# Attention and two MLPs on one core: the second q's pieces over five units, and the weight conversions' buffers

## The chip, the cores and the metric

The kernel runs on one core of a Trainium2 chip. Its time is the device time of one execution in microseconds (us); lower is better. The engines are named as in the profile: PE (TensorE, matmul) with PEld (its weight loads), DVE (VectorE), ACT (ScalarE), POOL (GpSimd) and SP (SyncE, which here only issues DMAs).

## The reference, cut to what matters

```python
q, k, v: (4, 8, 576, 64)                       # batch, heads, sequence, head size
q_rot, k_rot = rotate(q), rotate(k)            # x1*cos - x2*sin, x1*sin + x2*cos
scores = q_rot @ k_rot.T / 8
attn = exp(scores - max(scores));  attn = attn / (sum(attn) + 1e-9)
x = (attn @ v), heads side by side             # (2304, 512)
h = x @ w_in                                   # (512, 2048), float64 in memory
g = where(h >= 1, h, where(h <= -1, 0, (h + 1)**2 / 4));  x = g @ w_out
h = x @ w_in2;  g = s * max(h, 0)**2 + b;      out = g @ w_out2
```

## The kernel before

**Precision.** Matmuls run on a rounded 32-bit format, and each operand is split into a high part (rounded) and a low part (the rest), so that a product is three matmuls: high by high, high by low, low by high. The weights of both MLPs come as 64-bit floats. `convert` makes the two parts out of a half slice of 128x512: ACT scales the upper words into the tile `wa` (L134); four DVE instructions (L135 to L138) build the 32-bit word in `wm` and the scaled rest in `wa`; ACT rounds `wm` into the high part (L139); POOL then takes `wm` minus the high part, written back to `wm`, and adds `wa` into the low part. A helper cuts each POOL operation into two pieces of 256 columns (all have line 96). `wa` and `wm` have one buffer each, the raw words (`wraw`) have two.

**Attention.** It runs over 16 pairs of heads, each of 9 units, so over units 0 to 143. A unit is: PE makes the scores (L357, `sc`), DVE takes their negated maximum (L359, `nm`), ACT takes the exponential (L364, `p`), PE transposes `p` (L379, `tp`), ACT or DVE copies that out (`pt`), PE multiplies by v (L405, `av`). Per pair, `rope_pair` rotates the q and the k of the next pair: POOL multiplies by the table (`qin<-qin,tab_sb`, `kin<-kin,tab_sb`), DVE or POOL adds, `lay_q` (ACT L308 and DVE L309) writes q's high and low parts into `qs`, and the k goes by DMA. For q of the second pair (pair 1) the rotation is DVE's (L292, L294), in two halves of 288 columns at units 2 and 3. The result of a pair is written in two groups to `u` (two buffers) and stored with one DMA.

**The fill.** From unit 48 on, matmuls of the first MLP (`h`, `y`, L181) on batches that are done stand between the units. The conversions for them are asked for from unit 33 on (every second unit) and from unit 70 on (every fourth), and may move up to 14 units earlier; from unit 96 on, eight more are parked in memory. After the attention follow the rest of the first MLP (`hps`, `yps`) and the second one (`sum`, `yps`).

**What sets the order.** During the attention a scheduler puts the instructions of each engine in a fixed order when the program is built, from its own idea of their durations; an engine then works through its list strictly in that order. `issue_after` ties an instruction behind another one of the same engine. After the attention PE's order is the order of the code.

Of the kernel before, what the change touches and what calls it, by code (L numbers as in the profile page):

```python
# [8 lines left out]
F32 = mybir.dt.float32  # L9
# [5 lines left out]
ALU = mybir.AluOpType  # L15
# [4 lines left out]
B, H, S, D = 4, 8, 576, 64  # L20
# [3 lines left out]
P = 128  # L24
NP = H // 2
# [41 lines left out]
def kernel(ctx, tc, qq, kk, vv, tab, ww1, ww2, s, b, out):  # L67
# [28 lines left out]
            m = nc.gpsimd.tensor_tensor(out=out[c], in0=in0[c], in1=in1[c], op=op)  # L96
        return m

    made = []

    def split(dst_hi, dst_lo, src, hi_eng, lo_eng):
        if hi_eng is nc.scalar:
# [12 lines left out]
    class Slice:  # L115
# [6 lines left out]
        def convert(self, raw, pools, hi, lo):  # L122
            if not wide:
                split(hi, lo, raw, nc.scalar, nc.gpsimd)
                return


            top = raw.bitcast(F32).rearrange("p (n t) -> p n t", t=2)[:, :, 1]
            low = raw.bitcast(U16).rearrange("p (n t) -> p n t", t=4)[:, :, 1]
            pool = pools[self.f * 2 + self.made & 1 if len(pools) > 1 else 0]  # L130
            a = pool.tile([P, HW], F32, tag="wa", name="wa", bufs=WB)
            m = pool.tile([P, HW], F32, tag="wm", name="wm", bufs=WB)
            au, mu = a.bitcast(U32), m.bitcast(U32)
            nc.scalar.activation(a, top, AF.Copy, scale=2.0 ** -112)  # L134
            nc.vector.tensor_scalar(out=mu, in0=au, scalar1=3, scalar2=None, op0=ALU.logical_shift_left)  # L135
            nc.vector.scalar_tensor_tensor(out=mu, in0=au, scalar=0x80000000, in1=mu, op0=ALU.bitwise_and, op1=ALU.bitwise_or)
            nc.vector.tensor_scalar(out=au, in0=mu, scalar1=0xFF800000, scalar2=None, op0=ALU.bitwise_and)
            nc.vector.scalar_tensor_tensor(out=a, in0=low, scalar=2.0 ** -36, in1=a, op0=ALU.mult, op1=ALU.mult)  # L138
            nc.scalar.copy(hi, m)  # L139
            pool_tt(out=m, in0=m, in1=hi, op=ALU.subtract)  # L140
            pool_tt(out=lo, in0=m, in1=a, op=ALU.add)

        def load(self, stage, k):
            raw = stage.tile([P, HW], self.ww.dtype, tag="wraw", name="wraw", bufs=RB)
# [94 lines left out]
    g1p = p1.enter_context(tc.tile_pool(name="g1p", bufs=GB1, reuse_waits="tile"))  # L239
    att = pa.enter_context(tc.tile_pool(name="att", bufs=1, side="right", reuse_waits="tile"))  # L240
    att2 = pa.enter_context(tc.tile_pool(name="att2", bufs=2, side="right", reuse_waits="tile"))
    ps_s = pp.enter_context(tc.tile_pool(name="ps_s", bufs=2, space=PSUM))
    ps_b = pp.enter_context(tc.tile_pool(name="ps_b", bufs=4 - BF, space=PSUM))
    ps_f = pp.enter_context(tc.tile_pool(name="ps_f", bufs=BF, space=PSUM)) if BF else ps_b
# [180 lines left out]
    def finish(i, g, e, eb, slices):  # L425
        ps = bank("av")
        for kts in slices:
            av(i, g, ps, kts)
            if 3 not in kts:
                yield  # L430
        rm = bank("rm")
        for t in range(2):
            nc.tensor.transpose(rm[:, t * P:(t + 1) * P], eb[:, 2 * t:2 * t + 2, :].rearrange("p j d -> p (j d)"), ident)
        if g == 0:
            nc.tensor.transpose(rm[:, 256:384], e[:, 4:5].to_broadcast([P, P]), ident)
            u_t[i] = att2.tile([P, S], F32, tag="u", name="u")
        r = att2.tile([P, 384], F32, tag="r", name="r", bufs=1)
        nc.scalar.copy(r[:, :384 - 128 * g], rm[:, :384 - 128 * g])
        u = u_t[i]
        c = slice(256 * g, 256 * g + 256)  # L440
        nc.vector.tensor_tensor(out=u[:, c], in0=ps[:, :256], in1=r[:, :256], op=ALU.mult)
        if g == 0:
            nc.vector.tensor_tensor(out=u[:D, 512:], in0=ps[:D, 256:320], in1=r[:D, 256:320], op=ALU.mult)
            nc.vector.tensor_tensor(out=u[D:, 512:], in0=ps[D:, 256:320], in1=r[D:, 320:384], op=ALU.mult)
            return
        bb, hp = divmod(i, NP)
        nc.sync.dma_start(out=xd[hp, :, bb * S:(bb + 1) * S], in_=u_t.pop(i))
# [26 lines left out]

    kept, begun = set(), set()

    def beside(work):
        x = split_x(work[0][0], work[0][0] in kept)
        for _ in range(LEAD):
            yield 1.0  # L480
        for n, (c, gi) in enumerate(work):
            grp = set_a[gi * G1:(gi + 1) * G1]
            gs = []
            for sl in grp:
                while sl.made < 1:
                    sl.half(wst, scratch)
                ps = ps_f.tile([P, 512], F32, tag="bank", name="h")
                accumulate(ps[:, :N1], h_terms(sl.w, *x), CF)
                gs.append(act1(ps[:, :N1], N1, ac1, g1p, nc.vector if c < GE else nc.gpsimd))
                if c not in kept:  # L490
                    kept.add(c)
                    keep_parts(x, c * N1, N1)
                yield 1.0
            if n + 1 < len(work) and work[n + 1][0] != c:
                x = split_x(work[n + 1][0], work[n + 1][0] in kept)
            for sl in grp:
                while sl.made < 2:
                    sl.half(wst, scratch)
            for d in range(KD):
                at = slice(c * N1, (c + 1) * N1)  # L500
                if c in begun:
                    yq = m2.tile([P, N1], F32, tag="yq", name="yq", bufs=2)
                    nc.sync.dma_start(out=yq, in_=yd[0, d, :, at])
                ps = ps_f.tile([P, 512], F32, tag="bank", name="y")
                accumulate(ps[:, :N1], y_terms([sl.w for sl in grp], gs, d), CF)
                y = m2.tile([P, N1], F32, tag="ys", name="ys")
                nc.scalar.copy(y, ps[:, :N1])  # L507
                if c in begun:
                    pool_tt(out=yq, in0=y, in1=yq, op=ALU.add)
                    y = yq  # L510
                nc.sync.dma_start(out=yd[int(c in begun), d, :, at], in_=y)
                yield 1.0
            begun.add(c)
# [71 lines left out]
    def do_load(n):  # L585
# [10 lines left out]
        if n < len(units):  # L596
            i, k = units[n]
            if i + 1 < NPAIR:
                if i == 0 and k in (2, 3):
                    with tc.issue_after(maxs[k]):  # L600
                        rope_pair(1, "q", nc.vector, nc.vector, None, HALVES[k - 2:k - 1])
                if i and k == 0:
                    with ExitStack() if i > 1 else tc.issue_after(parts[1][1]), ExitStack() if i > 1 else tc.issue_after(maxs[8]):
                        rope_pair(i + 1, "q", nc.gpsimd, nc.vector, None)
                elif k == 2:
                    with ExitStack() if i else tc.issue_after(exps[2]), ExitStack() if i else tc.issue_after(lowest):
# [24 lines left out]
    def do_av(n):  # L631
# [7 lines left out]
        while todo:  # L639
            i, k, steps = todo[0]  # L640
            with tc.issue_after(tps[n - LT]) if n < NS else ExitStack():
                more = next(steps, True)
            if more is None:
                if n < NS:
                    break
                continue
            todo.pop(0)
            if k == 8 and (i + 1) % NP == 0 and i // NP < B - 1:
                fill.append(beside(ORDERS[i // NP]))

    def do_fill(n):
        if n < 48:
# [10 lines left out]
                acts[o](n)  # L663
    while fill:
        run_fill(1.0)
    pa.close()
    pp.close()
    p1.close()
# [532 lines left out]
```

## Time and profile before

| | us |
|---|---|
| runs | 1116.85, 1114.28, 1115.39 |
| median | 1115.39 |
| the profiled execution: time | 1117.7 |
| the profiled execution: span from first to last instruction | 1115.9 |
| PE busy in the span | 1076.5 (96%) |
| DVE, ACT, POOL busy | 779.3, 629.0, 428.1 |
| attention and fill on PE end at about | 442 |

The profiled execution is 2.3 us above the median. PE's idle time lies almost entirely in the first 280 us and in the last few. A PE that is shown busy is not a PE at its peak, since the ends of matmuls are modelled. The granted clock is TensorE's, as a share of its higher level.

### The profile page before, as it was taken

How to read it: one execution, taken by the hardware profiler on the slowest of the kernel's cores; microseconds unless marked ns; L12 is line 12 of the kernel's file. 1: busy time of each engine (PE TensorE's matmuls, PEld its weight loads, DVE VectorE, ACT ScalarE, POOL GpSimd, SP SyncE). 2: the span in 40 equal slices, each digit the busy share in tenths (PEclk: the TensorE clock that was granted, in tenths of full speed). 3: DMA queues.
4: the chain of work that ended last, by engine and by line, in shares of the span. 5: the costliest groups of instructions: out<-in, count | busy, mean ns of one | idle time of the engine just before them, and what ended most of it. 6: DMA issues, size and time to landing. Idle time of an engine off the chain costs nothing.

```text
span 1115.9 us, 20048 instructions
## 1 busy us (share of the span) xinstructions
PE 1076.5 (96%) x7296; PEld 983.0 (88%) x7296; DVE 779.3 (70%) x1453; ACT 629.0 (56%) x1432; POOL 428.1 (38%) x564
## 2 busy tenths in 40 slices
PE   3999999989999999999999999999999999999998
PEld 3776778868888889999999999999999999999997
DVE  7889987878676663444757667866787778677754
ACT  5677776767666665554545455474554448334431
POOL 6889987676473232332544445110212110000000
PEclk9999999999999999999999999999999999999999
DMA  8466856656675554645455663231322844221210
GB/s 240 146 194 178 256 169 204 187 161 205 203 228 161 171 165 134 224 171 187 151 180 207 213 226 122 91 108 64 113 90 90 303 158 127 83 82 43 80 63 36
DMA packets 109762, 173.24 MB, mean 155 GB/s; under 512 B 29408, under 2 KB 80608, under 8 KB 109664
## 3 DMA queue, kind: packets, MB, share of 16 engines
q1 hardware_dynamic: 109664, 171.97, 48.4%
q8 instruction: 57, 0.93, 0.4%
q14 instruction: 41, 0.34, 0.1%
HBM read 110.10 MB, written 48.56 MB: 142 GB/s over the span
## 4 chain that ended last, share of the span: by engine, by line
PE 83%; DVE 6%; ACT 3%; POOL 3%; issue 2%; DMA 2%; SPq 0%; POOLq 0%; ACTq 0%
PE hps L181 15%; PE sum L937 14%; PE yps L853 6%; PE yps L852 6%; PE yps L851 6%; PE y L181 5%; PE sc L357 5%; PE av L405 5%; PE yps L787 4%; PE yps L788 4%; PE yps L789 4%; PE h L181 4%; PE tp L379 3%; DVE nm L359 1%; POOL kin L96 1%
## 5 line engine op out<-in xcount | busy, mean ns | idle before, releaser
L181 PE MATMUL hps<-xh,w 128*128 128x288 f32 (+4 forms) x640 | 163.4, 324 | 0.0
L357 PE MATMUL sc<-kh,qs 128*128 128x288 f32 x336 | 103.1, 329 | 23.5 <-ACT p L364 13.2
L364 ACT ACTIVATE p<-sc,nm 128x576 f32<-128x576 f32 x144 | 106.5, 741 | 31.5 <-DVE nm L359 28.9
L359 DVE TENSOR_REDUCE nm<-sc 128x1 f32<-128x576 f32 x144 | 106.6, 749 | 25.0 <-PE sc L357 24.5
L945 ACT ACTIVATE four<-four,b_sb,s_sb 128x480 f32<-128x480 f32 x64 | 47.4, 782 | 126.5 <-DVE four L944 126.5
L853 PE MATMUL yps<-gh,w 128*128 128x480 f32 (+1 forms) x320 | 118.5, 370 | 0.0
L851 PE MATMUL yps<-gh,w 128*128 128x480 f32 (+1 forms) x320 | 118.4, 370 | 0.0
L852 PE MATMUL yps<-gl,w 128*128 128x480 f32 (+1 forms) x320 | 118.4, 370 | 0.0
L96 POOL TENSOR_TENSOR wm<-wm,w 128x256 f32<-128x256 f32 x80 | 69.0, 883 | 119.7 <-ACT w L139 62.8
L181 PEld LDWEIGHTS hps<-xh,w 128*128 128x128 f32 x640 | 113.3, 188 | 1.0
L181 PE MATMUL hps<-xl,w 128*128 128x288 f32 (+4 forms) x320 | 103.7, 324 | 0.0
L357 PEld LDWEIGHTS sc<-kh,qs 128*128 128x128 f32 x336 | 63.9, 193 | 42.8 <-ACT p L364 22.3
L357 PE MATMUL sc<-kz,qs 128*128 128x288 f32 x336 | 94.2, 302 | 0.0
L787 PE MATMUL yps<-gh,w 128*128 128x288 f32 (+3 forms) x288 | 93.0, 323 | 0.8 <-ACT ys L507 0.5
L788 PE MATMUL yps<-gl,w 128*128 128x288 f32 (+3 forms) x288 | 92.8, 322 | 0.0
L789 PE MATMUL yps<-gh,w 128*128 128x288 f32 (+3 forms) x288 | 92.8, 322 | 0.0
L379 PE MATMUL tp<-ident,p 128*128 128x128 f32 x576 | 88.3, 278 | 4.1 <-DVE pt L386 3.6
L96 POOL TENSOR_TENSOR wm<-wm,raw 128x256 f32<-128x256 f32 x16 | 12.8, 817 | 176.4 <-ACT raw L139 176.4
L379 PEld LDWEIGHTS tp<-ident,p 128*128 128x128 f32 x576 | 70.7, 143 | 7.6 <-DVE pt L386 4.3
L181 PE MATMUL y<-gh,w 128*128 128x288 f32 x320 | 74.1, 302 | 2.0 <-DVE ptr L397 0.9
L405 PE MATMUL av<-pt,vin 128*64 128x256 f32 (+1 forms) x512 | 75.6, 420 | 0.0
L181 PE MATMUL h<-xh,w 128*128 128x288 f32 x320 | 73.2, 305 | 2.2 <-ACT pt L384 1.6
(154 smaller groups left out, 2886.3 us busy)
## 6 DMA issues: line engine op xcount, KB each, us to landing
wraw<-in_ww SPq DMA_DIRECT2D x56, 512.0 KB, 4.2
w<-parkd SPq DMA_DIRECT2D x24, 512.0 KB, 5.7
kin<-in_k SPq DMA_DIRECT2D x15, 576.0 KB, 5.1
qin<-in_q SPq DMA_DIRECT2D x15, 576.0 KB, 4.4
kh<-kin SPq DMA_DIRECT2D x60, 144.0 KB, 2.7
parkd<-wraw SPq DMA_DIRECT2D x16, 512.0 KB, 3.0
xs<-y1d SPq DMA_DIRECT2D x32, 240.0 KB, 2.6
xd<-u SPq DMA_DIRECT2D x16, 288.0 KB, 2.6
```

Of the source, the lines that this page charges most:

```text
L181: m = nc.tensor.matmul(out_ps, l, r, start=(i == 0), stop=(i == n - 1))
L357: nc.tensor.matmul(sc[:, half, o:o + n], l, r[:, k0:k0 + n], start=m == 0, stop=m == len(todo) - 1)
L359: maxs[i * 9 + k] = nc.vector.tensor_reduce(out=nm, in_=sc[:, :, :288], axis=AX.XY, op=ALU.max, negate=True).ins
L379: m = nc.tensor.transpose(v[:, c, :], p[:, c * P:(c + 1) * P], ident)
L405: nc.tensor.matmul(ps[j * D:(j + 1) * D, :n], v[:, kt, j, :], pt[g][:, kt, j, :], start=kt == 0, stop=False)
L787: nc.tensor.matmul(acc, wh, gh, start=f == 0, stop=False)
L788: nc.tensor.matmul(acc, wh, gl, start=False, stop=False)
L789: nc.tensor.matmul(acc, wl, gh, start=False, stop=last)
L851: nc.tensor.matmul(acc, wh, gh, start=f == 0, stop=False)
L852: nc.tensor.matmul(acc, wh, gl, start=False, stop=False)
L853: nc.tensor.matmul(acc, wl, gh, start=False, stop=last)
L937: nc.tensor.matmul(acc, l, r, start=j == 0, stop=j == len(t) - 1)
```

## The change

Three things change. (1) Pair 1's q: the first half is turned at unit 2 as before, but laid out head by head at units 4 and 5; the second half is turned at unit 6 and laid out at units 7 and 8. (2) In `convert` the difference goes to the low part's place and the scaled word is added there, so that `wm` is read for the last time one POOL operation earlier. (3) During the attention `wa` comes in turn from two pools, so it has two buffers; `u` has one instead of two. After the attention `wa` has one buffer again.

```diff
-            a = pool.tile([P, HW], F32, tag="wa", name="wa", bufs=WB)
+            beside.reverse()
+            a = (beside or [pool])[0].tile([P, HW], F32, tag="wa", name="wa", bufs=WB)
             m = pool.tile([P, HW], F32, tag="wm", name="wm", bufs=WB)
...
             nc.scalar.copy(hi, m)
-            pool_tt(out=m, in0=m, in1=hi, op=ALU.subtract)
-            pool_tt(out=lo, in0=m, in1=a, op=ALU.add)
+            pool_tt(out=lo, in0=m, in1=hi, op=ALU.subtract)
+            pool_tt(out=lo, in0=lo, in1=a, op=ALU.add)
...
+    beside.extend((att2, wst))
...
-            u_t[i] = att2.tile([P, S], F32, tag="u", name="u")
+            u_t[i] = att2.tile([P, S], F32, tag="u", name="u", bufs=1)
...
-                if i == 0 and k in (2, 3):
+                if i == 0 and k in (2, 6):
                     with tc.issue_after(maxs[k]):
-                        rope_pair(1, "q", nc.vector, nc.vector, None, HALVES[k - 2:k - 1])
+                        turned_by(qk_in["q", 1], HALVES[k // 6])
+                if i == 0 and k in (4, 5, 7, 8):
+                    with tc.issue_after(maxs[k]), tc.issue_after(exps[k - 1]):
+                        lay_q(1, qk_in["q", 1], HALVES[k // 6], None, [int(k in (5, 8))])
                 if i and k == 0:
-                    with ExitStack() if i > 1 else tc.issue_after(parts[1][1]), ExitStack() if i > 1 else tc.issue_after(maxs[8]):
+                    with ExitStack() if i > 1 else tc.issue_after(parts[1][1]), ExitStack() if i > 1 else tc.issue_after(maxs[9]):
...
     while fill:
         run_fill(1.0)
+    beside.clear()
```

The scheduler's order changes with it through the whole attention. Three places follow. In the first, DVE, units 3 to 6 (each `nm<-sc` is a unit's maximum; `qs_108` is the laid out q of pair 1; `qin` its input), before:

```order
L359 TENSOR_REDUCE nm<-sc 128x1
L292 TENSOR_TENSOR qin<-qin,tab_sb 128x2x288
L386 COPY pt<-tp 128x4x128
L309 SCALAR_TENSOR_TENSOR qs_108<-qin,qs_108 64x288 x2
L294 TENSOR_TENSOR qin<-qin 128x288
L359 TENSOR_REDUCE nm<-sc 128x1 x2
L309 SCALAR_TENSOR_TENSOR qs_108<-qin,qs_108 64x288
L386 COPY pt<-tp 128x4x128
L309 SCALAR_TENSOR_TENSOR qs_108<-qin,qs_108 64x288
```

and now, from the same maximum of unit 3 on:

```order
L361 TENSOR_REDUCE nm<-sc 128x1
L388 COPY pt<-tp 128x4x128
L361 TENSOR_REDUCE nm<-sc 128x1
L311 SCALAR_TENSOR_TENSOR qs_108<-qin,qs_108 64x288
L361 TENSOR_REDUCE nm<-sc 128x1
L388 COPY pt<-tp 128x4x128
L311 SCALAR_TENSOR_TENSOR qs_108<-qin,qs_108 64x288
L361 TENSOR_REDUCE nm<-sc 128x1
L532 TENSOR_TENSOR qin<-qin,tab_sb 128x2x288
L422 RECIPROCAL sume<-sume 128x5
L399 COPY ptr<-tr 128x384
L361 TENSOR_REDUCE nm<-sc 128x1
```

Between the maxima of units 3 and 4 stood a multiplication, two layouts and an addition; there only a copy is left. The four moved instructions stand up to six maxima later; by the maximum of unit 11 both orders hold the same work.

The second place is POOL at the first two conversions (`wm<-wm,w` or `w<-wm,w` is the difference, `w<-wm,wa` or `w<-w,wa` the sum; `kin`, `qin`, `vin`, `eb` belong to the attention). Before:

```order
L96 TENSOR_TENSOR kin<-kin,tab_sb 128x2x144 x4
L96 TENSOR_TENSOR wm<-wm,w 128x256 x2
L275 MEMSET vin 64x64
L422 COPY eb<-sume 128x256
L96 TENSOR_TENSOR kin<-kin 128x288
L275 MEMSET vin 64x64
L96 TENSOR_TENSOR kin<-kin 128x288
L96 TENSOR_TENSOR w<-wm,wa 128x256 x2
L96 TENSOR_TENSOR kin<-kin 128x288 x2
L422 COPY eb<-sume 128x256
L96 TENSOR_TENSOR qin<-qin,tab_sb 128x2x144 x4
L96 TENSOR_TENSOR kin<-kin,tab_sb 128x2x144 x4
```

and now:

```order
L96 TENSOR_TENSOR w<-wm,w 128x256 x2
L96 TENSOR_TENSOR kin<-kin,tab_sb 128x2x144 x4
L96 TENSOR_TENSOR w<-w,wa 128x256
L277 MEMSET vin 64x64
L96 TENSOR_TENSOR w<-w,wa 128x256
L424 COPY eb<-sume 128x256
L96 TENSOR_TENSOR kin<-kin 128x288
L277 MEMSET vin 64x64
L96 TENSOR_TENSOR kin<-kin 128x288
L96 TENSOR_TENSOR w<-wm,w 128x256 x2
L96 TENSOR_TENSOR w<-w,wa 128x256
```

The second conversion's difference came after the next pair's `qin` and `kin` products; now it stands before them. Counted over DVE's whole order by the first of a conversion's four instructions, conversions begin at units 19, 28, 37, 41 and 47 before, and at 19, 23, 28, 31, 35, 38, 44 and 47 now; from there to unit 98 at 54, 58, 63, 66, 70, 74, 78, 82, 84, 90, 92 and 94 before, and at 54, 57, 60, 64, 68, 73, 76, 80 and 92 now. From unit 99 on they stand at the same units.

The third place is ACT from the exponential of unit 84 on (`p,sums<-sc,nm` is a unit's exponential, `ac`, `gh` belong to the fill). Before:

```order
L364 ACTIVATE p,sums<-sc,nm 128x576
L203 ACTIVATE ac<-ac 128x288
L103 CAST gh<-h 128x288
L438 COPY r<-rm 128x256
L134 ACTIVATE wa<-wraw 128x512
L202 ACTIVATE ac<-h 128x288
L203 ACTIVATE ac<-ac 128x288
L384 COPY pt<-tp 128x4x128
L364 ACTIVATE p,sums<-sc,nm 128x576
L139 CAST w<-wm 128x512
```

and now:

```order
L366 ACTIVATE p,sums<-sc,nm 128x576
L103 CAST gh<-h 128x288
L440 COPY r<-rm 128x256
L203 ACTIVATE ac<-h 128x288
L204 ACTIVATE ac<-ac 128x288
L386 COPY pt<-tp 128x4x128
L366 ACTIVATE p,sums<-sc,nm 128x576
```

The conversion's two instructions are gone from there; they stand at earlier units. PE's order holds the same matmuls, with the fill at nearly the same units, and is the same from its 1578th matmul on.

## Rows read from the trace of the kernel before

**Rows 1.** The page: busy time, share of the span, instructions of each engine.

```profile
PE 1076.5 (96%) x7296; PEld 983.0 (88%) x7296; DVE 779.3 (70%) x1453; ACT 629.0 (56%) x1432; POOL 428.1 (38%) x564
```

**Rows 2.** Windows: stretch, us; busy PE, PEld, DVE, ACT, POOL; clock, DMA share, GB/s.

```profile
14.07:36.29 22.22, 15.68 (x81) 12.90 (x81) 19.79 (x28) 13.28 (x32) 17.24 (x22) 0.85 0.65 201
56.06:73.65 17.59, 17.36 (x130) 12.48 (x131) 16.19 (x29) 13.56 (x34) 13.63 (x18) 1.00 0.65 190
73.65:92.43 18.78, 18.78 (x137) 12.99 (x136) 17.16 (x29) 14.68 (x35) 17.88 (x24) 1.00 0.64 184
92.43:114.02 21.59, 19.91 (x144) 14.02 (x144) 19.80 (x33) 16.76 (x40) 19.16 (x26) 1.00 0.64 182
...
56.06:119.48 63.42, 61.51 (x447) 43.17 (x448) 57.93 (x99) 48.97 (x116) 55.86 (x73) 1.00 0.66 192
119.48:276.58 157.10, 143.31 (x1084) 123.19 (x1081) 125.22 (x216) 112.05 (x274) 120.51 (x160) 0.99 0.63 193
276.58:398.99 122.41, 120.46 (x937) 107.58 (x937) 82.67 (x155) 83.13 (x206) 56.43 (x82) 1.00 0.65 199
442.16:1115.90 673.74, 668.89 (x4270) 642.62 (x4269) 451.50 (x879) 327.17 (x699) 141.68 (x171) 1.00 0.41 135
```

**Rows 3.** Timeline, DVE and one PE row: start, us, instruction, [idle before, releaser].

```profile
20.51 0.75 DVE L359 TENSOR_REDUCE nm<-sc 128x1 f32<-128x576 f32 x1
21.18 0.90 DVE L292 TENSOR_TENSOR qin<-qin,tab_sb 128x576 f32<-128x576 f32 x1
...
22.71 2.06 DVE L309 SCALAR_TENSOR_TENSOR qs<-qin,qs 64x288 fp32r<-64x288 f32 x2
24.80 0.93 DVE L294 TENSOR_TENSOR qin<-qin 128x288 f32<-128x288 f32 x1
25.66 1.41 DVE L359 TENSOR_REDUCE nm<-sc 128x1 f32<-128x576 f32 x2
...
27.59 0.61 PE L357 MATMUL sc<-kh,qs 128*128 128x288 f32 x1 [3.91 <-ACT p L364]
...
31.19 0.76 DVE L359 TENSOR_REDUCE nm<-sc 128x1 f32<-128x576 f32 x1 [0.38 <-PE sc L357]
32.26 0.56 DVE L397 COPY ptr<-tr 128x384 f32<-128x384 f32 x1 [0.31 <-PE tr L395]
34.18 0.76 DVE L359 TENSOR_REDUCE nm<-sc 128x1 f32<-128x576 f32 x1 [1.37 <-PE sc L357]
```

**Rows 4.** Tiles `wa` and `wm` to 460 us: count, ns least/median/most, first and last start.

```profile
L135 DVE TENSOR_SCALAR wm<-wa x24: 416/594/1144, 59.0 to 395.8; 128x512 uint32<-128x512 uint32 x24
L136 DVE SCALAR_TENSOR_TENSOR wm<-wa,wm x24: 666/691/1186, 61.0 to 396.2; 128x512 uint32<-128x512 uint32 x24
L137 DVE TENSOR_SCALAR wa<-wm x24: 410/428/1052, 63.0 to 396.9; 128x512 uint32<-128x512 uint32 x24
L138 DVE SCALAR_TENSOR_TENSOR wa<-wraw,wa x24: 653/694/1236, 64.3 to 397.9; 128x512 f32<-128x512 uint16 x24
...
L96 POOL TENSOR_TENSOR wm<-wm,w x32: 719/732/1292, 70.7 to 256.6; 128x256 f32<-128x256 f32 x32
```

**Rows 5.** Waits to 445 us: total us, times, longest.

```profile
ACT wa L134 <- POOL w L96: 14.8, 7, 5.1
```

**Rows 6.** Timeline of the longest of these waits: POOL, ACT, then PE.

```profile
226.07 3.08 POOL L96 TENSOR_TENSOR qin<-qin,tab_sb 128x288 f32<-128x288 f32 x4 [3.41 <-DMA qin<-in_q]
229.11 1.95 POOL L96 TENSOR_TENSOR w<-wm,wa 128x256 fp32r<-128x256 f32 x2
...
231.09 0.68 ACT L134 ACTIVATE wa<-wraw 128x512 f32<-128x512 f32 x1 [5.06 <-POOL w L96]
...
233.07 0.40 PE L181 MATMUL h<-xh,w 128*128 128x288 f32 x1 [1.56 <-ACT pt L384]
...
237.19 0.66 PE L379 MATMUL tp<-ident,p 128*128 128x128 f32 x4 [1.74 <-DVE pt L386]
```

**Rows 7.** The page: issues of one DMA, count, size, median us to landing.

```profile
xd<-u SPq DMA_DIRECT2D x16, 288.0 KB, 2.6
```

More of the change, by code (lines that the diff above doesn't have):

```diff
@@ L97, in pool_tt @@
         return m
-    made = []
+    made, beside = [], []
     def split(dst_hi, dst_lo, src, hi_eng, lo_eng):
@@ L475, with share @@
     kept, begun = set(), set()
-    def beside(work):
+    def share(work):
         x = split_x(work[0][0], work[0][0] in kept)
@@ L648, in do_av @@
             if k == 8 and (i + 1) % NP == 0 and i // NP < B - 1:
-                fill.append(beside(ORDERS[i // NP]))
+                fill.append(share(ORDERS[i // NP]))
     def do_fill(n):
```

## The prediction

> **What bounds the kernel now.** I read the page first, then windows over the stretches of the program, then the list of waits, then the timeline at two places. The page shows PE busy for 1076.5 of 1115.9 us [rows 1], so at most some 39 us can be won without less matmul work. The windows say where they lie. After 442.16 us PE is busy 668.89 of 673.74 us [rows 2]; there the change leaves PE's order alone, and what it moves on other engines is covered by PE. So the time is decided in the attention, and that has three kinds of stretch. From 56.06 to 119.48 (units 18 to 47, before any fill) DVE is busy 57.93 of 63.42 us, 91%, and POOL 55.86 [rows 2]: the side engines set the pace, since each unit needs DVE's maximum before ACT's exponential. From 119.48 to 276.58 (units 48 to 98, with fill and most conversions) PE is idle 157.10 - 143.31 = 13.8 us. From 276.58 to 398.99 (more fill, fewer conversions) it is idle only 1.95 of 122.41 us [rows 2]. Every unit follows the one before, so a delay in any of the three reaches the end, unless PE has other work standing in line.
>
> Durations below come from one profiled execution of 1117.7 us (span 1115.9); I add the change to that and take off 2.3 us for the median of the runs, 1115.4.
>
> **The change part by part.**
>
> *Pair 1's q.* Between the maxima at 20.51 and 25.66 DVE does the second half's product (0.90), the first half's two layouts (2.06) and the second half's addition (0.93), 3.9 us in all. The scores that wait for the exponential behind the second maximum start at 27.59 after 3.91 us of PE idle, and the granted clock of that pair is 0.85 [rows 3, 2]. In the new order only the copy stands there, so units 4 to 8 come 3 to 4 us earlier. But by the maximum of unit 11 the same instructions have been done in both orders, and DVE was busy nearly throughout; it can come out earlier there only by the idle it had: 0.38 + 0.31 + 1.37 = 2.06 us [rows 3]. What is late next is DVE itself. Bounds: 0 (the scores find the next pair's k not there yet) and 3.9; I take -2.1, the idle.
>
> *The second buffer of `wa`.* Before, ACT's first step of a conversion had to wait for POOL's sum of the conversion before; seven such waits cost ACT 14.8 us, and behind each stand exponentials [rows 5]. The longest, 5.06 us, was followed by PE gaps of 1.56 and 1.74 us [rows 6]. With two buffers that step needs the sum of two conversions back. But the scheduler uses the freedom at once: up to unit 47 eight conversions start instead of five, and from unit 48 to 98 nine instead of twelve, none between units 81 and 91. So three chains of DVE work move out of the stretch where PE sets the pace, into the one where DVE does.
>
> Early, that costs: a chain is four DVE instructions, 594 + 691 + 428 + 694 ns = 2.41 us by the medians, 2.15 by the least and 4.62 by the most [rows 4]. Lower end: DVE's idle in the stretch, 5.49 us [rows 2], swallows all but 3 x 2.15 - 5.49 = 1.0 us. Upper end: the pair from 92.43 holds two chains and takes 21.59 us, the two pairs before it hold one each and take 17.59 and 18.78 [rows 2], so another chain costs up to 21.59 - 18.2 = 3.4 us (the pair also splits some tokens), 10.2 for three. I take the medians, 3 x 2.41 = +7.2 us, because idle at 91% busy is mostly the short waits between dependent steps and hard to use.
>
> In the middle, that pays: were PE idle there at the later stretch's rate, 1.95 / 122.41 = 1.6%, 2.5 of the 13.8 us would remain, so 11.3 us is the most. I keep the 3.3 us of [rows 6] out of it: there POOL had first waited 3.41 us for the DMA of q, and that wait isn't touched. I take -8.0; the lower end is 0, if the gaps find another releaser.
>
> *The difference in the low part's place.* No operation is added: the two pieces cost 732 ns each whichever place they are written to [rows 4]. The gain is that `wm` is free one sum earlier. This makes a new wait possible: with two `wa`, DVE's first step of a conversion now waits for POOL's difference of the one before, and the next maximum is queued behind it. Before, ACT's wait for the sum always came first. I count it inside the early price; it is what the second rival is made of.
>
> *`u` with one buffer.* The store takes 2.6 us [rows 7]; the next pair's first write comes five units later, some 9.8 us at 17.59 us for nine [rows 2]. Nothing, unless SP is late by 7 us.
>
> *After the attention.* The same instructions with `wa` single again, under a PE that is 99% busy [rows 2]: 0. If that cover were missing, the earlier release of `wm` would still not cost.
>
> Sum: -2.1 + 7.2 - 8.0 = -2.9 us. Profiled execution 1114.8, median 1115.4 - 2.9 = 1112.5.
>
> **The rivals.** (a) *The early stretch pays more than the middle gives back.* DVE and POOL are both about nine tenths busy there, each of three more conversions adds four pieces of at least 0.72 us to POOL [rows 4], and DVE's first step can stand still until POOL has made the difference, with the maximum behind it. At 3.4 us a chain, and a middle that gives back only 5 us since the DMA waits of q stay: +10.2 - 2.1 - 5.0 = +3.1, median 1118.5. With the full 8.0 it decides from (8.0 + 2.1) / 3 = 3.4 us a chain. For it: one DVE step of a conversion took 1144 ns where another took 416 [rows 4]. The Trainium skill ("SBUF — State Buffer", Who interferes with whom) says that a DVE instruction in a two-port mode, or with two inputs in SBUF, and a reading POOL instruction exclude each other for a whole instruction, whichever started first; the spread of that row agrees with it. By that rule alone, taking every chain at the most of its rows, the early price would be 3 x 4.62 = 13.9 us, and the sum +3.8. Against it: the medians lie near the least.
>
> (b) *It cancels.* The scheduler starts each conversion as soon as it believes a buffer free, and POOL on the chip runs behind that belief, so the waits come back two conversions later and the second buffer doesn't do what it is named for. The middle gives 4.6 us: +7.2 - 2.1 - 4.6 = +0.5, median 1115.9.
>
> (c) *Nearly all is won.* The early chains fit into DVE's idle (+1.0), the middle gets to the later stretch's rate (-11.3), the q pieces bring 2.1: -12.4, median 1103.0. Against it: it needs DVE at almost 100% in the early stretch.
>
> **How the numbers follow.** 0.2%, about what a measurement of this kernel can tell from no change, is 2.2 us. The forecast (1112.5, for itself 1107 to 1113.2) has 0.38, (c) 0.10, (b) 0.22, (a) 0.30. Faster is the forecast and (c), 0.48; the same is (b), 0.22; slower is (a), 0.30. Both signs are well held, because the sum is a small difference of two terms of 7 and 8 us, each uncertain by 3. For the range I leave out most of (c) and the end of (a) where the early price passes its bound: 1106 to 1120.
>
> **What would show it.** In the changed kernel's profile: PE's gap of 3.91 us near 27.6 gone, the maximum of unit 4 near 22 us and the one of unit 11 about 2 us earlier than before (right), or not earlier (the first step is wrong). Unit 47 later by about 7.2 - 2.1 = 5 us, with DVE busier than 91% from unit 18 on. ACT's waits for POOL's sum shrunk from 14.8 us to a few, and PE's idle between units 48 and 98 near 6 us instead of 13.8. If DVE now shows waits of several us for POOL's difference, (a) is under way; if ACT still waits some 10 us for the sum, (b). If PE shows new gaps after 442 us, or `u` waits for its store, the parts that I cost at nothing were wrong.

## The result, and the profile after

| | us |
|---|---|
| changed kernel, runs | 1123.37, 1125.67, 1123.19, 1125.30 |
| changed kernel, median | 1124.34 |
| kernel before beside it, median of 4 | 1114.92 |
| ratio, 95% interval | 1.0086 (1.0073 to 1.0099) |
| profiled executions of the changed kernel | 1123.4 and 1122.8 |

The changed kernel is slower by 9.4 us; the forecast was 1112.5, with a range to 1120.

The execution of before that the forecast rests on took 1117.7 us, at the upper end of that kernel's runs. A second profile of the same kernel (`before_again`, 1115.0) is nearer to their median, and the stretches below are compared with it. The page of the changed kernel, first row, to be read beside [rows 1]: PE does the same work, so what was lost is idle.

```profile
PE 1075.6 (96%) x7296; PEld 984.2 (88%) x7296; DVE 784.2 (70%) x1453; ACT 627.6 (56%) x1432; POOL 432.8 (39%) x564
```

Windows of `before_again` and then of the changed kernel, columns as in [rows 2]. Each runs from the maximum of one unit to that of the next named: units 4, 18, 45, 48, 72, 99, then to the end of the last `y` (the fill's last matmul; in the first profile of the kernel before it ends at 454.7, past the 442 that its table gives), then to the end.

```profile
25.27:55.74 30.47, 28.54 (x180) 20.22 (x181) 24.81 (x40) 21.71 (x52) 27.35 (x35) 0.89 0.53 153
55.74:113.24 57.50, 55.59 (x406) 39.55 (x407) 53.04 (x89) 45.04 (x107) 51.08 (x66) 1.00 0.66 183
113.24:118.72 5.48, 5.48 (x43) 3.68 (x43) 4.81 (x12) 3.96 (x10) 5.00 (x7) 1.00 0.77 245
118.72:185.02 66.30, 60.94 (x469) 52.12 (x465) 56.80 (x95) 49.16 (x121) 54.19 (x72) 1.00 0.70 209
185.02:273.44 88.42, 81.02 (x619) 69.52 (x615) 69.14 (x123) 62.24 (x154) 66.79 (x88) 1.00 0.60 184
273.44:451.99 178.55, 176.51 (x1370) 157.57 (x1368) 106.48 (x207) 114.37 (x290) 70.03 (x101) 1.00 0.58 182
451.99:1113.23 661.24, 656.40 (x4177) 630.43 (x4176) 446.46 (x866) 319.12 (x675) 137.71 (x166) 1.00 0.41 133
```

```profile
23.08:54.01 30.93, 27.30 (x192) 19.20 (x191) 28.36 (x43) 22.50 (x54) 29.20 (x38) 1.00 0.60 175
54.01:114.90 60.89, 54.74 (x395) 38.27 (x393) 58.95 (x98) 46.51 (x109) 57.20 (x70) 1.00 0.66 190
114.90:123.51 8.61, 8.61 (x73) 6.68 (x73) 6.34 (x14) 5.52 (x12) 8.53 (x12) 1.00 0.75 219
123.51:197.27 73.76, 63.70 (x475) 54.91 (x473) 61.22 (x101) 50.88 (x124) 62.53 (x80) 0.95 0.63 190
197.27:279.67 82.40, 76.87 (x585) 68.20 (x584) 59.79 (x107) 58.03 (x145) 53.28 (x72) 0.98 0.58 179
279.67:458.29 178.62, 176.60 (x1373) 157.99 (x1371) 106.14 (x206) 113.92 (x289) 69.57 (x101) 1.00 0.59 180
458.29:1121.56 663.27, 657.25 (x4177) 630.29 (x4176) 448.77 (x866) 318.81 (x675) 138.90 (x166) 1.00 0.40 132
```

Read the idle of PE, length minus busy. The lengths alone mislead, because the fill does not lie at the same place between two maxima: units 72 to 99 look 6.0 us shorter, but hold 585 matmuls instead of 619.

| stretch | idle, before_again | idle, changed | difference |
|---|---|---|---|
| units 4 to 18 | 1.93 | 3.63 | +1.7 |
| 18 to 48 | 1.91 | 6.15 | +4.2 |
| 48 to 72 | 5.36 | 10.06 | +4.7 |
| 72 to 99 | 7.40 | 5.53 | -1.9 |
| 99 to the last `y` | 2.04 | 2.02 | 0.0 |
| to the end | 4.84 | 6.02 | +1.2 |

That is 9.9 us more idle and, from 1065.08 - 1064.48, 0.6 us more busy time, less the 2.2 us by which unit 4 comes earlier: 8.3 us, the difference of the two spans. The second profile of the changed kernel has the same shape.

Two of the new gaps show how it comes about. At the first fill (ACT, then PE, then SP's issues; in brackets the idle before and what ended it):

```profile
126.08 0.43 ACT L103 CAST xh<-xs 128x288 fp32r<-128x288 f32 x1 [5.24 <-DMA xs<-xd]
126.42 0.73 ACT L366 ACTIVATE p<-sc,nm 128x576 f32<-128x576 f32 x1
...
127.30 0.40 PE L359 MATMUL sc<-kh,qs 128*128 128x288 f32 x1 [3.12 <-ACT p L366]
...
115.60 0.54 SPq L264 DMA_DIRECT2D qin<-in_q  x1
119.99 0.33 SPq L264 DMA_DIRECT2D kin<-in_k  x1
120.37 0.42 SPq L146 DMA_DIRECT2D wraw<-in_ww  x1
120.85 1.51 SPq L473 DMA_DIRECT2D xs<-xd  x3
```

The first input of the fill (`xs`) is asked for behind a k and behind the raw words of one more conversion. The k takes the longest: SP had ended the issue before it at 116.14 and sent the k at 119.99; the raw words then cost half a microsecond. ACT's cast of it stands in ACT's list ahead of the exponential of unit 48, whose maximum had ended at 124.25 (its start, 123.51, is a window's edge above). In `before_again` the first of the three loads goes out ahead of the k, and ACT waits 1.15 us:

```profile
114.00 0.33 SPq L471 DMA_DIRECT2D xs<-xd  x1
...
117.77 0.33 SPq L262 DMA_DIRECT2D kin<-in_k  x1
118.14 0.90 SPq L471 DMA_DIRECT2D xs<-xd  x2
...
119.27 0.43 ACT L103 CAST xh<-xs 128x288 fp32r<-128x288 f32 x1 [1.15 <-DMA xs<-xd]
```

At 161 us the fill's `y` waits for `gl`, and on DVE two steps of a conversion and two maxima stand in line ahead of it:

```profile
158.14 0.43 DVE L136 TENSOR_SCALAR wm<-wa 128x512 uint32<-128x512 uint32 x1 [0.17 <-ACT wa L135]
158.49 0.75 DVE L361 TENSOR_REDUCE nm<-sc 128x1 f32<-128x576 f32 x1
159.15 0.93 DVE L137 SCALAR_TENSOR_TENSOR wm<-wa,wm 128x512 uint32<-128x512 uint32 x1
160.00 0.74 DVE L361 TENSOR_REDUCE nm<-sc 128x1 f32<-128x576 f32 x1
160.67 0.44 DVE L107 TENSOR_TENSOR gl<-h,gh 128x288 fp32r<-128x288 f32 x1
...
161.17 0.40 PE L182 MATMUL y<-gh,w 128*128 128x288 f32 x1 [2.29 <-DVE gl L107]
```

Behind either gap the granted clock falls to the lower level, 1.2 GHz, for some 3 us (windows of two microseconds; the clock is the third number from the end):

```profile
128.00:130.00 2.00, 1.51 (x8) 1.11 (x7) 2.00 (x4) 1.97 (x6) 2.00 (x3) 0.52 0.99 350
130.00:132.00 2.00, 2.00 (x13) 1.98 (x13) 2.00 (x4) 0.93 (x3) 2.00 (x4) 0.62 0.28 50
...
162.00:164.00 2.00, 2.00 (x12) 1.99 (x11) 1.94 (x3) 2.00 (x6) 2.00 (x3) 0.56 0.84 201
164.00:166.00 2.00, 2.00 (x12) 2.00 (x10) 1.97 (x2) 1.81 (x5) 2.00 (x3) 0.59 0.07 12
```

### The profile page after: what moved, and what is told of

Read it like the earlier page. It is cut to its first block, busy times and chain, and to the rows that moved or that the text cites. A ratio compares the mean times of both kernels' runs of the same rounds, so it can differ in the third digit from the quotient of the medians.

```text
span 1121.6 us, 20041 instructions
## 1 busy us (share of the span) xinstructions
PE 1075.6 (96%) x7296; PEld 984.2 (88%) x7296; DVE 784.2 (70%) x1453; ACT 627.6 (56%) x1432; POOL 432.8 (39%) x564
## 4 chain that ended last, share of the span: by engine, by line
PE 65%; DVE 14%; DMA 8%; ACT 5%; issue 4%; POOL 3%; SPq 0%; DVEq 0%; POOLq 0%; ACTq 0%
PE sum L943 13%; PE hps L182 10%; PE yps L858 6%; PE yps L859 6%; PE yps L857 6%; PE h L182 4%; PE sc L359 4%; PE y L182 4%; PE av L407 3%; DVE nm L361 3%; PE tp L381 3%; PE yps L793 2%; PE yps L794 2%; PE yps L795 2%; DMA qin<-in_q 2%
## 5 line engine op out<-in xcount | busy, mean ns | idle before, releaser
L96 POOL TENSOR_TENSOR w<-wm,w 128x256 fp32r<-128x256 f32 x80 | 71.2, 911 | 125.4 <-ACT w L140 125.1
L96 POOL TENSOR_TENSOR raw<-wm,raw 128x256 fp32r<-128x256 f32 x16 | 12.8, 818 | 174.9 <-ACT raw L140 152.1
```

## The experiments

### Each part alone, and the conversions held at their old units

Theory A: the loss comes from the three chains that moved ahead of unit 48, and only the low part's place and the second buffer together move them.

`q_only`, the kernel before with:

```diff
-                if i == 0 and k in (2, 3):
...
+                if i == 0 and k in (2, 6):
...
+                if i == 0 and k in (4, 5, 7, 8):
```

> The kernel before with pair 1's q pieces spread over units 2 to 8, nothing else; its order starts five conversions before unit 48 (19, 27, 33, 39, 46), as before. Theory A (crowding: the loss comes from the eight conversions that start before unit 48 when the low part's place and the second wa buffer come together): unit 9 about 3.3 us earlier, unit 18 about 2, and 1 to 2 us of it reach the end: 1113 to 1114. Theory B (the gain of the q pieces is always given back, because DVE was busy anyway): 1115, unit 27 no earlier than before (73.65).

Measured: 1116.5, ratio 1.0014 (1.0000 to 1.0028), later than either theory said. The early gain is there (the maximum of unit 9 at 32.01 instead of 36.04), and by unit 48 (119.89 instead of 118.72) it is gone.

`l_only`, the kernel before with:

```diff
-            pool_tt(out=m, in0=m, in1=hi, op=ALU.subtract)
-            pool_tt(out=lo, in0=m, in1=a, op=ALU.add)
+            pool_tt(out=lo, in0=m, in1=hi, op=ALU.subtract)
+            pool_tt(out=lo, in0=lo, in1=a, op=ALU.add)
```

> The kernel before with the difference written to the low part's place, nothing else; five conversions before unit 48 (19, 28, 36, 43, 47). Theory A (crowding): unit 48 within 1 us of before (119.5), unit 99 too. Theory C (the place itself costs, above all after the attention, where the changed kernel lost 2.2 us of PE between 458 us and the end of the last h): about 1117, with PE gaps of over 1 us in all after 455 us where before had 0.8. If the place costs nothing anywhere: 1115.

Measured: 1118.6, ratio 1.0034 (1.0022 to 1.0047). Theory A said nothing would be lost; 3.8 us are, with the conversions all but in their old places. Nor are they lost where theory C looked first: from the end of the last `y` on PE is idle 4.98 us in this profile, 4.84 in `before_again`.

`w_only`, the kernel before with:

```diff
+            beside.reverse()
+            a = (beside or [pool])[0].tile([P, HW], F32, tag="wa", name="wa", bufs=WB)
...
+    beside.extend((att2, wst))
...
+            u_t[i] = att2.tile([P, S], F32, tag="u", name="u", bufs=1)
```

> The kernel before with a second wa buffer during the attention (and one u), nothing else; wm is still read by POOL's sum; five conversions before unit 48 (19, 28, 35, 39, 46), eleven from 48 to 91. Theory A (crowding): no loss before unit 48, ACT's 14.8 us of waits for the sum gone, so 1111 to 1115. Theory D (a second buffer lets DVE's first step stand behind POOL, with the maximum behind it, wherever the conversions are): 1118 to 1121, with DVE waiting for POOL's sum some 5 to 10 us in all.

Measured: 1117.1, ratio 1.0016 (1.0002 to 1.0029). This is the run that decides on the forecast's largest gain. ACT's list of waits in `before_again` has the row below (the profile of before had 14.8 us, [rows 5]); in `w_only` that row is gone altogether:

```profile
ACT wa L134 <- POOL w L96: 11.9, 6, 5.2
```

And the windows of `w_only` over units 48 to 72 and 72 to 99:

```profile
120.36:189.02 68.66, 61.51 (x463) 52.64 (x464) 58.78 (x97) 50.41 (x123) 56.69 (x75) 0.98 0.69 207
189.02:274.95 85.93, 80.35 (x613) 70.51 (x610) 68.98 (x120) 60.17 (x151) 65.04 (x84) 0.98 0.59 183
```

PE is idle 7.15 + 5.58 = 12.73 us there; in `before_again` 5.36 + 7.40 = 12.76. All of ACT's waits for the sum are removed, and PE's idle is the same; the two profiles of the kernel before differ by 1.0 us in it. Other waits have come up, ACT's for the raw words, which have two buffers as before, and DVE's for POOL's sum (3.4 and 4.5 us of the totals below lie between units 48 and 99):

```profile
ACT wa L135 <- DMA wraw<-in_ww: 5.6, 4, 2.1
DVE wm L136 <- POOL w L96: 4.7, 5, 1.9
```

The second row is theory D at about the size that it named; its 1118 to 1121 is missed by a microsecond. So the run shows that removing ACT's waits for the sum brings PE nothing. It does not show whether they had cover or only gave way to these.

`held`, the changed kernel with its conversions tied to units (`EM`: 33, 35, 37, 41, 47, 54 and so on, where they are asked for; `BU`: 19, 28, 37, 41, 47, 54 and so on, as in the kernel before):

```diff
-        if n in range(33, 51, 2) or n in range(70, 110, 4):
-            with tc.issue_after(exps[n - 14]):
+        if n in EM:
+            with tc.issue_after(exps[BU[EM.index(n)] - 1]):
```

> The changed kernel with its conversions tied to the units at which they start in the kernel before (19, 28, 37, 41, 47, then 53 to 92). Theory A (crowding): the early loss is gone, unit 48 at 116 to 119 instead of 123.5, the middle a few us shorter than before's 157.1, time 1110 to 1115. Theories C and D (the place or the second buffer cost by themselves): 1120 to 1124, as the changed kernel.

Measured: 1126.6, ratio 1.0106 (1.0093 to 1.0120), slower than the changed kernel itself. From unit 18 to 48 the early loss is smaller, as theory A said: PE's idle is 2.74 us there, where the changed kernel has 6.15.

```profile
55.37:120.93 65.56, 62.82 (x464) 44.78 (x462) 60.45 (x103) 49.16 (x116) 54.44 (x71) 1.00 0.66 194
```

But units 48 to 99 take 161.02 us, with 17.8 us of idle. That does not decide against theory A, because the tie costs time of its own: `q_held` below has the same tie without the low part's place and the second buffer, and takes 7.5 us more than `q_only`. What falls, with `l_only`, is theory A's claim that the parts cost nothing while the conversions stay where they were.

### Pairs of parts, and the kernel before once more

Theory E: the parts' costs add up. Theory F: only the low part's place and the second buffer together cost.

`lw`, the changed kernel with pair 1's q as before:

```diff
-                if i == 0 and k in (2, 6):
...
+                if i == 0 and k in (2, 3):
```

> The changed kernel with pair 1's q pieces put back to units 2 and 3; seven conversions start before unit 48 (19, 25, 29, 35, 39, 44, 47). Theory E (the parts add up: low part's place +3.8, second buffer +2.3, q pieces +1.7 us by their medians): 1121. Theory F (the low part's place and the second buffer cost only together, since together they let a conversion start while POOL is still on the one before): 1122 to 1126, that is nearly all of the changed kernel's 9.4 us.

Measured: 1121.2, ratio 1.0051 (1.0034 to 1.0067), what the sum of the two parts gives.

`ql`, the changed kernel without the second buffer:

```diff
-    beside.extend((att2, wst))
...
-            u_t[i] = att2.tile([P, S], F32, tag="u", name="u", bufs=1)
+            u_t[i] = att2.tile([P, S], F32, tag="u", name="u")
```

> The changed kernel with one wa buffer and two u; five conversions before unit 48 (19, 27, 33, 39, 46). Theory E (parts add up): 1120. Theory F (only the pair of low part's place and second buffer costs): 1115 to 1118.

Measured: 1117.9, ratio 1.0023 (1.0013 to 1.0033).

`qw`, the changed kernel with the difference back in `wm`:

```diff
-            pool_tt(out=lo, in0=m, in1=hi, op=ALU.subtract)
-            pool_tt(out=lo, in0=lo, in1=a, op=ALU.add)
+            pool_tt(out=m, in0=m, in1=hi, op=ALU.subtract)
+            pool_tt(out=lo, in0=m, in1=a, op=ALU.add)
```

> The changed kernel with the difference back in wm; five conversions before unit 48 (19, 26, 34, 38, 45). Theory E (parts add up): 1119. Theory F (only the pair of low part's place and second buffer costs): 1114 to 1117.

Measured: 1115.8, ratio 1.0009 (0.9996 to 1.0021).

Neither theory holds whole. Theory F's ranges have `ql` and `qw`, and its 1122 for `lw` is still inside that run's interval, but `l_only` had lost 3.8 us without the second buffer. Theory E holds for `lw` (0.34% + 0.16% against 0.51%), not for the pairs with q (0.48% against 0.23%; 0.30% against 0.09%), nor for all three (0.64% against 0.86%). By the medians no part gains, and what the low part's place costs depends on what else is in the order: 0.34% alone, 0.09% beside the q pieces (`ql` against `q_only`, not clear of noise), 0.77% beside both other parts (the changed kernel against `qw`).

Read together, the orders without the tie leave theory A's crowding open. Where five conversions start before unit 48 (`q_only`, `l_only`, `w_only`, `ql`, `qw`) the time is 1115.8 to 1118.6; with seven (`lw`) it is 1121.2, with eight (the changed kernel) 1124.3. The order moves more of them forward where the low part's place and the second buffer are together, so no run here parts the crowding from those two; the one that was to, `held`, has the tie, and the tie costs by itself.

`before_again`, unchanged:

> The kernel before, unchanged, for a second profile of it. Its profiled execution took 1117.7 us, above nearly all of its other runs (median 1114.8). If the halved clock after PE's longer idle times makes the difference between its runs, this execution, at about 1114.8, shows a granted clock of 0.996 to 0.998 instead of 0.995, and lacks one of the two stretches at half clock (26 to 34 us and 183 to 188 us). If it lacks neither, the spread comes from elsewhere.

As expected: 1115.0 us, clock 0.996. It has the half clock behind the gap near 27 us (0.89 in its first window above), and not the one that the first profile shows at 183 to 187 us, behind a gap of 1.92 us at 182.11; here that gap is 1.65 us, at 180.35. Some 1 us of idle in units 48 to 99 (13.8 against 12.76) and that stretch of half clock were the first execution's alone.

### The fill's first input, the waits taken late, and the changed kernel once more

`xs_late`, the changed kernel with:

```diff
-        if n < 48:
+        if n < 51:
             return
-        with tc.issue_after(exps[min(n, len(units)) - 4]):
-            run_fill(0.62 if n < 76 else 0.92)
+        with tc.issue_after(exps[50 if n == 51 else min(n, len(units)) - 4]):
+            run_fill(4 * 0.62 if n == 51 else 0.62 if n < 76 else 0.92)
```

> The changed kernel with its fill begun at unit 51 instead of 48 (with the share of four units at once), so that ACT's first casts of the fill's input, which waited 5.24 us for a DMA at 126.08 us with the exponential of unit 48 queued behind them, stand behind unit 50's exponential. Conversions nearly as in the changed kernel (19, 23, 28, 31, 35, 38, 44, 48). Theory H (that wait, the PE gap of 3.12 us at 127.3 and the half clock from 128 to 132 us behind it are a good part of the loss): gap gone, clock 1.00 around 128, 1119 to 1121. Theory E (the conversions' DVE and POOL work itself sets the pace there, the wait only shows where): 1123 to 1125.

`before_xs_late`, the same edit in the kernel before:

> The control for xs_late: the same later begin of the fill in the kernel before, where ACT waited only 0.7 to 1.2 us for that DMA. Both theories: 1114 to 1117. If it also gains 4 us (1111), the later begin is good by itself and says nothing of the changed kernel.

Measured: `xs_late` 1120.6, ratio 1.0054 (1.0033 to 1.0076), as theory H said; the control 1117.7, ratio 1.0028 (1.0015 to 1.0041), just above both theories. The later begin costs 2.8 us in the kernel before and brings 3.8 us in the changed one, so if the later begin by itself costs the same in both, the wait for the fill's input and what hangs on it was worth some 6 us of the 9.4; by the intervals it can be 3 or 10. The windows of `xs_late` for units 45 to 48 and 48 to 72:

```profile
114.04:119.81 5.77, 5.77 (x49) 4.34 (x50) 5.73 (x13) 4.93 (x11) 5.69 (x8) 1.00 0.77 213
119.81:190.34 70.53, 61.71 (x464) 52.50 (x460) 61.35 (x97) 51.14 (x129) 66.33 (x84) 0.98 0.72 212
```

Unit 48 comes at 119.81 instead of 123.51, in part because less of the fill stands before it (49 matmuls in the first window instead of 73). The stretch after it still holds 8.82 us of idle, where the changed kernel has 10.06: a gap of 2.30 us is now at 130.82, with 3 us at the lower clock behind it. The gain of 3.8 us is not shown as idle at that one place.

`wlate`, the kernel before with the lines of `w_only`, but with the second buffer in use only for the conversions asked for from unit 70 on:

```diff
+        if n == 70:
+            beside.extend((att2, wst))
```

> The kernel before with the second wa buffer only for the conversions asked for from unit 70 on (and one u); the order up to unit 70 is that of before. In before ACT waits 10 us for POOL's sum between units 72 and 99. If these waits lie on the path: those units take some 5 us less than 88.4, time 1110. If the waits are only where ACT stands while DVE and POOL set the pace (in w_only they were all gone and the time was no better): 85 to 88 us there, time 1113 to 1116.

Measured: 1115.1, ratio 1.0005 (0.9992 to 1.0018); ACT's waits for the sum in units 72 to 99 are gone, and those units take 87.89 us, with PE idle for 6.5 us of them (`before_again`: 88.42 and 7.40). That is the second outcome that was foreseen, without the change of the earlier order that `w_only` has: taking the waits away is not worth 5 us. Here too others came up, ACT's for the raw words (4.3 us) and DVE's for the sum (2.2).

`after_again`, the changed kernel unchanged:

> The changed kernel, unchanged, for a second profile. If the losses of the first one are the order's and not that execution's: ACT waits 4 to 6 us for the fill's input near 126 us, PE has a gap of 2.5 to 3.5 us near 127 with the clock at a half behind it, units 48 to 72 take 72 to 75 us (before: 66.3 and 68.1), and the part after 459 us is some 2 us longer than before's. If the loss sits at other places this time, the places are chance and only the sum is the order's.

Measured: 1122.8. ACT waits 4.50 us for the fill's input at 126.28, PE has its gaps of 2.36 us at 127.50 and 2.85 us at 160.77, units 48 to 72 take 72.41 us, the part after the last `y` 662.36. So the gaps belong to the order. The half clock does not follow each of them: here it comes behind the gaps at 40.48 and 160.77, and once near 290, not behind the one at 127.50.

### The part after the attention, and two more orders

`tail_old`, the changed kernel with the difference back in `wm` once the attention is over:

```diff
+            d = lo if beside else m
+            pool_tt(out=d, in0=m, in1=hi, op=ALU.subtract)
+            pool_tt(out=lo, in0=d, in1=a, op=ALU.add)
```

> The changed kernel with the difference written back to wm in every conversion after the attention (the attention as changed). Theory T1 (after the attention the low part's place costs: both profiles of the changed kernel lose 1.2 to 2.2 us there): 1122 to 1123, and the distance to the kernel before stays the same from the last h to the end. Theory T2 (what is lost there depends on how the attention is left, not on the place: kernels with the old place lose 0.8 to 1.1 us there too, others nothing): 1124, and 1 to 2 us still lost after the last h.

Measured: 1123.9, ratio 1.0080 (1.0065 to 1.0094). Its windows of a stretch in the attention and of the part after the last `y`:

```profile
130.00:142.00 12.00, 10.59 (x49) 8.12 (x50) 10.11 (x15) 8.30 (x20) 11.86 (x17) 0.57 0.56 166
462.98:1123.56 660.58, 656.27 (x4176) 630.40 (x4176) 446.72 (x866) 318.54 (x675) 138.21 (x166) 1.00 0.41 133
```

In this profile the last part is as short as before (660.58 against 661.24), which speaks for T1; by the medians nothing is won. `w_only`, with the old place throughout, has 662.43 there, so the place is not the whole cause. What the 1 to 2 us after the attention are stays open.

`held_again`, unchanged:

> The kernel of the run held, unchanged, for a second profile. In the first one DVE's addition for q at 124.72 us took 4.94 us instead of 0.74 while POOL ran its pieces back to back, and PE then stood 4.69 us at 131. If the order brings this about each time: an addition of over 3 us near 124 and a PE gap of over 3 us near 131 again. If it was one meeting of the two engines by chance: an addition of about 1 us, units 48 to 54 some 4 us shorter, and the loss of about 10 us elsewhere.

Measured: 1127.0. The addition near 124 us is short this time; the long DVE instruction comes at 144.94 instead (4.37 us, shown in the last section), and the loss is as large. It belongs to this order, but not to one place.

`q_held`, `q_only` with the conversions tied as in `held`:

> The kernel before with pair 1's q pieces spread and the conversions tied to units not ahead of those of before; the order starts four before unit 48 (19, 28, 37, 45) instead of the five of q_only (19, 27, 33, 39, 46). Theory P (each chain before unit 48 costs 1 to 2 us there and q_only lost its early gain to chains moved forward): unit 9 3 to 4 us earlier than before, unit 48 about 2 us earlier; if the middle gives nothing back, 1112 to 1113, faster than both. Theory R (the chains left out come back at the same price later): 1115 to 1117.

Measured: 1124.0, ratio 1.0087 (1.0073 to 1.0101). Theory P falls: unit 9 is even earlier than it said (31.06), but one chain fewer before unit 48 doesn't save the gain. DVE waits for POOL's product of the next pair's q, the maximum of unit 11 is behind it, and the gap of 3.91 us that the spread pieces removed at 27 us is back at 42 (DVE, then PE):

```profile
38.48 1.33 DVE L295 TENSOR_TENSOR qin<-qin 128x576 f32<-128x576 f32 x1 [2.20 <-POOL qin L96]
41.00 0.74 DVE L360 TENSOR_REDUCE nm<-sc 128x1 f32<-128x576 f32 x1
...
42.66 0.61 PE L358 MATMUL sc<-kh,qs 128*128 128x288 f32 x1 [4.21 <-ACT p L365]
```

That brings unit 48 back to 119.62, 0.9 us behind `before_again`. The larger part of the 9.6 us is lost behind it. From unit 48 to 99, `q_only` and then `q_held`, with thirteen conversions each:

```profile
119.89:271.75 151.86, 139.63 (x1071) 120.78 (x1069) 126.31 (x215) 112.11 (x274) 121.25 (x158) 1.00 0.64 196
119.62:284.23 164.61, 145.58 (x1076) 124.96 (x1075) 130.38 (x219) 113.06 (x275) 121.12 (x163) 0.97 0.61 184
```

PE's idle is 12.2 us in the first and 19.0 in the second. The two kernels differ only in where the conversions are asked for and tied, so tying them down costs time without the other two parts, and `held` does it too.

## Why the prediction was wrong, by its own steps

*Pair 1's q, -2.1: right up to unit 18, not in the time.* The gap of 3.91 us at 27.6 [rows 3] is gone, unit 4's maximum starts at 23.08, and unit 18 comes 1.7 us earlier than in `before_again` (1.2 in the second profile). What was missed is that a smaller gap comes up at 41 (1.23 us here, 2.84 in the second profile), where the next pair's q now meets the pieces moved back; in `q_held` a gap there eats all of the gain. And by itself the part brought nothing: `q_only` is 1.7 us slower than the kernel before by the medians, and the changed kernel is faster without it (`lw`).

*Three chains more before unit 48, +7.2: right in kind, too high.* DVE is busy 58.95 of 60.89 us from unit 18 to 45, 97%, and POOL 57.20. PE's idle rises by 4.2 us, which is 1.4 a chain instead of 2.41: DVE's own idle took up more than assumed (from unit 18 to 45 it falls from 4.5 to 1.9 us). The forecast's lower bound had said it could.

*The middle, -8.0: the step that failed.* What it named as the means happened: ACT's waits for POOL's sum shrank from 14.8 us [rows 5] to 0.5,

```profile
ACT wa L135 <- POOL w L96: 0.5, 2, 0.3
```

and three chains left the stretch. But PE's idle between units 48 and 99 is 10.06 + 5.53 = 15.6 us, where the forecast had 6: instead of 8 us won, 1.8 are lost against the first profile and 2.8 against the second. The step took the time that ACT waits for time that PE loses. `w_only` and `wlate` show that it is not: with ACT's waits for the sum gone, in `wlate` those from unit 72 on, PE's idle between units 48 and 99 is 12.7 and 12.6 us, against 12.8. The likely reason is cover, that while ACT stood, DVE and POOL were doing the work that the next exponential needed; it is argued, since in both runs other waits took part of their place. The longest wait did stand beside two gaps of PE [rows 6], but a wait that ends just before a gap is not shown to be its cause. Only units 72 to 99, which lost chains, have less idle, by 1.9 us.

*What was costed at nothing.* The first fill: its input came late, with the exponential of unit 48 behind it. The PE gap alone is 2.4 to 3.1 us in the two profiles; `xs_late` and its control make it some 6, on the condition and with the interval given there. The raw words of the conversion moved ahead are half a microsecond of the delay on SP and the k the rest; why the k comes first in this order is not shown. The forecast had looked at which chains move, and not at what each of them then stands in front of on SP, ACT and DVE. After the attention: 1 to 2 us. `u` with one buffer: no wait for its store shows.

*Rival (a)* had the sign and part of the way (the early stretch pays, the middle gives too little back), but its mechanism is small: DVE waits for POOL's difference 2.9 us in two waits,

```profile
DVE wm L136 <- POOL w L96: 2.9, 2, 2.2
```

one of them (2.2 us, at 122.89) just ahead of unit 48's maximum. Its price for the early chains (10.2) is too high. (Against it the forecast says that the medians lie near the least; that of the first step, 594 ns against 416 [rows 4], does not.) It came to 1118.5 since it too let the middle give back 5 us. *Rival (b)* had the middle nearest to what was measured, for a wrong reason: the waits did not come back.

The low part's place alone costs 3.8 us (`l_only`). Why it costs so much with the conversions where they were is not settled, nor is how much of the whole loss is the crowding before unit 48.

## What to carry to other kernels

The total of an engine's waits is worth nothing until it is shown that the next engine runs dry because of them; take the wait away by itself before counting on it, as `w_only` did here for 0 of 8 us, and look at what waits come in its place. A run that ties an order down needs a control with the same tie, as `q_held` came to be for `held`. Where a scheduler packs side engines that are nine tenths busy, more buffers let it pull work forward, so look in the new order at what each pulled instruction now stands in front of, above all in front of the first load of the next stage. And profile the kernel before twice: here two executions of it differ by 2.7 us, about what the forecast was to find.

## What the runs showed of the hardware

A DVE instruction can last as long as a whole run of POOL instructions beside it. In `held` an addition that takes 0.74 to 1.35 us elsewhere in that run took 4.94 us. POOL ran six pieces back to back until 129.05 (126.02 + 3.03), and the addition ended 0.6 us behind that; the next maximum, the exponential and PE waited:

```profile
124.63 1.42 POOL L96 TENSOR_TENSOR w<-wm,w 128x256 fp32r<-128x256 f32 x2
124.72 4.94 DVE L296 TENSOR_TENSOR qin<-qin 128x576 f32<-128x576 f32 x1
126.02 3.03 POOL L96 TENSOR_TENSOR kin<-kin,tab_sb 128x288 f32<-128x288 f32 x4
...
131.31 0.61 PE L359 MATMUL sc<-kh,qs 128*128 128x288 f32 x1 [4.69 <-ACT p L366]
```

In `held_again` a step that took 0.42 to 1.14 us before [rows 4] took 4.37 us in the same way, and in `w_only` a layout at 181.31 took 3.13:

```profile
144.94 4.37 DVE L136 TENSOR_SCALAR wm<-wa 128x512 uint32<-128x512 uint32 x1
...
143.56 2.33 POOL L96 TENSOR_TENSOR qin<-qin,tab_sb 128x288 f32<-128x288 f32 x3
145.83 3.11 POOL L96 TENSOR_TENSOR kin<-kin,tab_sb 128x288 f32<-128x288 f32 x4
```

The Trainium skill ("SBUF — State Buffer", Who interferes with whom) says that where the two contend, DVE in a two-port mode or with two inputs in SBUF and POOL reading, whichever issues first holds the shared ports for its instruction, and the other blocks. A blocked DVE fits the rows; but the length does not stop at one instruction here, as if DVE got no turn between POOL's pieces. Neither profile of the kernel before shows such a case, and that it is the ports was not tried by itself.

The clock behind a gap is not the same from one execution to the next. Of the same order, the gap near 127 us was followed by 3 us at the lower level in one profile of the changed kernel and by none in the other. In `tail_old`, whose order in the attention is the same, the clock is 0.57 over 12 us (130 to 142, above) behind a gap of 3.33 us. It is a part of what runs of one kernel differ by: of the recorded runs of the kernel before, the 19 with a mean clock of 0.998 have a median of 1114.2 us and the 20 with 0.995 one of 1115.5. But runs of one mean clock, 0.996, still lie between 1111.9 and 1116.3, so the clock is not all of it, and the rest is not explained.
